# An allowance between a transfer's planned landing and its readers in the list schedule of a transformer block's end

## The chip, the cores and the metric

The kernel runs on one core of one Trainium2 chip. The metric is device time in microseconds (us), the median of several runs. The core's engines are TensorE (PE in the profile; its weight loads are PEld), VectorE (DVE), ScalarE (ACT), GpSimd (POOL) and SyncE (SP), which issues nearly all transfers (DMA). Each engine takes its instructions strictly in the order in which the program lists them, so an instruction that waits holds up everything behind it on its engine.

## The reference

One block with adaptive layer normalisation on a sequence of 2048 tokens of 512 features, all in float32: sliding-window attention (32 heads of 16, window 256), then a gated feed-forward layer of width 1792.

```python
mod = (_silu(c) @ w_mod).reshape(c.shape[0], 6, 1, -1)
sa, ca, ga, sb, cb, gb = (mod[:, i] for i in range(6))
h = _layernorm(x) * (1 + ca) + sa
x = x + ga * attention(h, wqkv, wo)        # 32 heads, causal, window 256, softmax
h = _layernorm(x) * (1 + cb) + sb
x = x + gb * ((_silu(h @ w1) * (h @ w3)) @ w2)
```

## The kernel before

Every float32 product is made of three reduced-precision products: each operand is split into a rounded part and the rest ("cutting": ScalarE copies the rounded part, VectorE or POOL subtracts it). Attention runs as 32 units (8 groups of four heads by 4 row blocks of 512 tokens), each laid out by a hand-made table of times. In a unit TensorE makes scores twice: once for the row maxima (L485 into the banks `mx`, reduced by VectorE at L494), once transposed for the probabilities (L753 into `st`); VectorE merges masks into a score tile (L773) or adds them (L761), ScalarE takes the exponential (L766, L768), POOL masks (L780), and TensorE multiplies by the values (L721). The maxima go back through DRAM-like rows (L517) into the queries' extra rows. A unit's sums and values leave through `os` (L815) to DRAM (L818, `o_dr`).

What comes after the planned time TS, the last units and all that follows, is not written out by hand. The function builds a list of operations, each with an engine, an assumed duration, a key and its dependences, and `Sched.deal` deals them out greedily: at every step it starts, over all engines, the operation that can start first, and on one engine the ready operation with the smallest key. The units' remaining operations are `fixed`: they take their engine at their planned times `us(t)`. The order in which `deal` picks is the order of the program; its times are used nowhere else. Its costs are constants: RATE (transfer speed) and QUIET (how close a transfer may come to an urgent one), TW (how planned unit times are stretched), PEM (an allowance between a result of ACT, DVE or POOL and its reader on TensorE) and DM. DM is an allowance between the landing of a transfer and its reader on any engine but SyncE, and holds only while fixed unit operations are left. `late` (in `deal`) selects these readers, and the last lines of the loop add the allowance:

```python
m = PEM if u.eng == "PE" and o.eng in ("ACT", "DVE", "POOL") else DM if late(o, u, s) else 0.0
u.est = max(u.est, s + (o.lat + m if u.eng != o.eng or o.kb else o.occ))
```

What is dealt, in the words of the prediction:

- Row sums (`o_sums`): for each row block the sums of 24 heads (tile `wqr`, 96 rows) and of the last 8 (tile `mT`, 32 rows) are loaded from `o_dr` (L1068), inverted by VectorE (L1072) and stored to `r_dr` (L1073).
- Pieces (`o_part`): four per row block. The values are loaded (L1092), the inverted sums are spread over them by a load (L1087), multiplied (L1104), rounded (L1096) and subtracted (L1099). `K["by"]` says for each piece whether VectorE or POOL multiplies and subtracts. The second row block's cut pieces lie in a tile named `x1b`, the others' in `o`.
- Projection (`o_proj`, L1116), the residual add with the row sum on VectorE (L985), the sum of squares on ScalarE (L993), the root on POOL (L1007).
- Normalised rows and their transposes for the first half of the tokens (L1236, L1250 on TensorE, L1254), and their sums, differences and cuts (L1267, L1273, L1275), which are the seven operands `b` of a Strassen-like product of 2 x 2 blocks.
- The feed-forward layer: 14 units (2 halves of the tokens by 7 slices). A unit has 14 *ups* (L1378, six matmuls each) with adds on VectorE and POOL (L1409, L1421), gates (L1401, L1405) and cuts (L1449, L1452), and 8 *downs* (L1471, six matmuls each) that VectorE adds to the residual (L1476). The weights are loaded by L1174 and cut by L967 and L968. The second half's normalised rows are transposed in between (L1302, L1311, L1315). The keys of all of it come from the table K.

Of the kernel before, what the change touches and what calls it, by code (L numbers as in the profile page):

```python
# [112 lines left out]
class Sched:  # L113
# [36 lines left out]
    def deal(self):  # L150
# [17 lines left out]
        while left:  # L168
            best = None
            for e, lst in ready.items():  # L170
                t, pick = free[e], None
                for key, seq, o in lst:
# [10 lines left out]
                    if o.kb:  # L183

                        b = max(s, t)
                        end = max(wire, b + 1.5) + o.kb / RATE + o.more - QUIET
                        s = max([s] + [u + 0.01 for u in self.urgent if b <= u < end])
# [36 lines left out]
            if o.kb:  # L224
                s = max(s, lanes.pop(0))
                wire = max(wire, s + 1.5) + o.kb / RATE + o.more
                o.lat = wire + 0.4 - s
# [17 lines left out]
            for u in o.users:  # L245
                m = PEM if u.eng == "PE" and o.eng in ("ACT", "DVE", "POOL") else DM if late(o, u, s) else 0.0
                u.est = max(u.est, s + (o.lat + m if u.eng != o.eng or o.kb else o.occ))
# [6 lines left out]

INORDER = ("up",)
INF = float("inf")
RATE = 320.0

QUIET = 1.487
KEY = 1.715  # L260
TS = 229.9

# [1 line left out]
def us(t):  # L264

    return KEY * (min(t, TW[0]) - TS + TW[2] * max(0.0, min(t, TW[1]) - TW[0]) + TW[3] * max(0.0, t - TW[1]))


TW = (231.0, 241.0, 0.8, 0.583)

KINDS = dict(product=("PE", 0.235), mix=("POOL", 1.25), qk_rows=("SP", 0.65), out=("ACT", 0.5), job=("POOL", 2.0),
             job_dma=("SP", 0.5), scores=("PE", 0.19), top=("DVE", 0.5), parts=("DVE", 0.4), turn=("PE", 0.11), cut=("ACT", 0.16),
# [1 line left out]
             far=("PE", 0.125), part=("POOL", 0.92), side=("ACT", 0.53), far_side=("ACT", 0.27), side_mask=("POOL", 0.92),  # L274
             side_probs=("ACT", 0.53), values=("PE", 0.66), cut_all=("ACT", 0.48), store=("SP", 0.45))
NPE = 3
PEM = 0.998
DM = 0.076

BY = ((("POOL", "POOL"),) * 3 + (("DVE", "DVE"),), (("POOL", "POOL"),) * 3 + (("DVE", "DVE"),),  # L280
      (("POOL", "DVE"),) * 3 + (("DVE", "DVE"),), (("POOL", "POOL"),) * 4)
K = dict(be=(('POOL', 'DVE'), ('POOL', 'DVE'), ('DVE', 'POOL'), ('POOL', 'POOL'), ('POOL', 'POOL'),
         ('POOL', 'POOL'), ('DVE', 'POOL')), hr=2.855, de=12.48, wo=-3.567, x1=16.6, xb=-38.041, xl=-26.167,
         os=-0.13, ol=(-17.833, -5.162, -9.509, 10.002), pl=(11.205, -2.398, -4.869, 102.62), pe=(0.914, -2.635,
         56.103, 231.635), o=(2.337, 8.384, 18.214, 9.324), n=(1, 1, 2, 1), w0=67.715, l2=2.802, f=2.068,
         fl=40.1, by=((('POOL', 'POOL'), ('DVE', 'DVE'), ('DVE', 'POOL'), ('DVE', 'DVE')), (('DVE', 'DVE'),
         ('DVE', 'POOL'), ('DVE', 'POOL'), ('DVE', 'DVE')), (('POOL', 'POOL'), ('DVE', 'DVE'), ('DVE', 'POOL'),
         ('POOL', 'DVE')), (('DVE', 'POOL'), ('DVE', 'POOL'), ('DVE', 'POOL'), ('DVE', 'POOL'))), w=-2.134,
         dn=1.412, ds=0.003, l3=-10.82)

@with_exitstack
def block_kernel(ctx: ExitStack, tc: tile.TileContext, x, wqk, wv, wo, w13, w2, c, wmod, out):
# [1313 lines left out]
```

## Time and profile before

| | us |
|---|---|
| median of 3 runs | 954.08 (952.42 to 954.97) |
| the profiled execution | 952.06 |
| its span, first to last instruction | 950.3 |
| TensorE busy in the span | 916.3 (96%) |
| VectorE, ScalarE, POOL busy | 670.0, 525.1, 545.6 |
| mean granted clock of TensorE | 0.982 |

In the rows below, a window's row gives its length, then for each engine its busy us (and instructions), the granted TensorE clock, the mean busy share of the 16 DMA engines and GB/s. A row in order of time gives start, duration, engine, line, operation, what it writes and reads, and in brackets how long the engine stood idle before it and what ended that. "SPq" is SyncE issuing a transfer.

### The profile page before, as it was taken

To read this page: it belongs to the slowest core of one execution; us is meant where nothing else is said; L and a number is where in the kernel's file an instruction comes from. 1 tells how busy PE (TensorE), PEld (TensorE's weight loads), DVE (VectorE), ACT (ScalarE), POOL (GpSimd) and SP (SyncE) were. 2 spreads that over 40 slices of the span, in tenths; PEclk is the share of its full clock that TensorE was granted. 3 is DMA by queue.
4 is the path that set the end of the run, shared out by engine and by line. 5 is a ranking of instruction groups with operands and counts; after the bars stand their busy time and mean duration, and the time that the engine had idled before them with its cause. 6 is when DMAs were issued, how large, how long until landed. Compare 5 with 4: busy or idle time off the path is not lost.

```text
span 950.3 us, 16719 instructions
## 1 busy us (share of the span) xinstructions
PE 916.3 (96%) x5330; PEld 710.3 (75%) x5330; DVE 670.0 (71%) x1861; ACT 525.1 (55%) x1031; POOL 545.6 (57%) x694
## 2 busy tenths in 40 slices
PE   5999999999999999988987999999999999999998
PEld 3688677777777777755765878888888888888886
DVE  7675789888898989876668565665558645566465
ACT  3333777777777777766577754333455334433330
POOL 6220566676757566645566789977659546453420
PEclk9999899999999999988989999999999999999999
DMA  8621465555655555565960659645244512323002
GB/s 296 200 80 46 113 185 163 158 146 164 183 156 150 170 157 147 136 183 167 298 220 12 221 199 322 222 171 166 90 161 157 187 41 99 99 62 97 26 23 89
DMA packets 125020, 141.62 MB, mean 149 GB/s; under 512 B 60034, under 2 KB 72834, under 8 KB 124932
## 3 DMA queue, kind: packets, MB, share of 16 engines
q1 hardware_dynamic: 124212, 139.51, 48.0%
q10 hardware_dynamic: 720, 1.05, 0.3%
q8 instruction: 42, 0.69, 0.3%
q14 instruction: 46, 0.38, 0.1%
HBM read 85.72 MB, written 34.61 MB: 127 GB/s over the span
## 4 chain that ended last, share of the span: by engine, by line
PE 78%; DVE 6%; DMA 4%; POOL 4%; ACT 3%; issue 2%; SPq 2%; POOLq 0%; DVEq 0%; ACTq 0%
PE st L1378 11%; PE mx L1378 10%; PE pj L438 8%; PE st L753 8%; PE mx L485 8%; PE po L721 8%; PE st L1471 7%; PE mx L1471 7%; PE st L653 5%; PE pj L1378 3%; PE pj L1471 2%; DMA r_dr<-mT 1%; DVE t L1267 1%; DVE b L1275 1%; DMA qk<-o_dr 1%
## 5 line engine op out<-in xcount | busy, mean ns | idle before, releaser
L494 DVE CUSTOM_DVE_ANT_0 junk<-mx,mskq 128x320 bf16<-128x320 f32 (+4 forms) x512 | 223.4, 464 | 39.6 <-PE mx L485 39.0
L968 POOL TENSOR_TENSOR w<-w,w 128x512 fp32r<-128x512 f32 (+2 forms) x56 | 107.0, 1924 | 111.6 <-ACT w L967 61.8
L485 PE MATMUL mx<-ringk,ringq 96*128 96x320 f32 (+4 forms) x512 | 154.9, 326 | 2.2 <-DVE mt L494 2.2
L753 PE MATMUL st<-ringq,ringk 98*128 98x256 f32 (+1 forms) x528 | 141.9, 338 | 6.8 <-DVE st L773 2.5
L780 POOL TENSOR_SCALAR_AFFINE_SELECT pt<-pt 128x256 f32<-128x256 f32 x224 | 92.4, 413 | 74.7 <-ACT pt L768 67.0
L438 PE MATMUL pj<-hT,wq 128*128 128x512 f32 x384 | 132.5, 403 | 0.3 <-DVE wq L427 0.3
L485 PEld LDWEIGHTS mx<-ringk,ringq 96*128 96x128 f32 x512 | 98.6, 193 | 41.4 <-DVE mt L494 23.1
L768 ACT ACTIVATE pt<-st 128x512 f32<-128x512 f32 (+1 forms) x198 | 115.2, 587 | 24.7 <-DVE st L773 10.5
L753 PEld LDWEIGHTS st<-ringq,ringk 98*128 98x128 f32 x528 | 91.8, 194 | 22.2 <-ACT pt L768 5.8
L721 PE MATMUL po<-pt,vS 128*17 128x384 f32 (+2 forms) x1408 | 92.7, 394 | 0.0
L438 PEld LDWEIGHTS pj<-hT,wq 128*128 128x128 f32 x384 | 68.4, 192 | 7.8 <-DVE wq L427 0.8
L1378 PE MATMUL st<-b,w 128*128 128x512 f32 x270 | 67.8, 391 | 1.3 <-ACT t L1412 1.3
L1409 DVE TENSOR_TENSOR t<-st,t 128x512 f32<-128x512 f32 x48 | 33.0, 688 | 43.3 <-PE st L1378 28.5
L1409 DVE TENSOR_TENSOR t<-mx,t 128x512 f32<-128x512 f32 x49 | 33.5, 687 | 41.8 <-PE mx L1378 28.0
L721 PEld LDWEIGHTS po<-pt,vS 128*17 128x17 f32 x1408 | 34.6, 98 | 36.3 <-issue 19.8
L1449 ACT ACTIVATE wq<-g 128x512 fp32r<-128x512 f32 x28 | 17.7, 631 | 77.2 <-DVE g L1405 38.1
L1378 PE MATMUL mx<-b,w 128*128 128x512 f32 x240 | 59.9, 389 | 0.0
L773 DVE COPY_PREDICATED st<-later,st 128x256 f32<-128x256 uint8 x112 | 47.5, 424 | 17.3 <-PE st L753 12.7
L1378 PEld LDWEIGHTS st<-b,w 128*128 128x128 f32 x270 | 50.5, 188 | 12.1 <-ACT t L1412 1.7
L795 POOL TENSOR_SCALAR_AFFINE_SELECT sm<-sm 128x256 f32<-128x256 f32 x109 | 42.3, 406 | 29.5 <-ACT sm L785 28.6
L761 DVE TENSOR_TENSOR st<-st,mskr 128x256 f32<-128x256 f32 x125 | 53.6, 429 | 8.0 <-PE st L753 8.0
L967 ACT ACTIVATE w<-w 128x512 fp32r<-128x512 f32 (+2 forms) x56 | 42.5, 786 | 20.7 <-DMA w<-wsum 11.2
(256 smaller groups left out, 2010.6 us busy)
## 6 DMA issues: line engine op xcount, KB each, us to landing
ringq<-qk SPq DMA_DIRECT2D x192, 64.0 KB
ringk<-qk SPq DMA_DIRECT2D x96, 128.0 KB
o_dr<-os SPq DMA_DIRECT2D x32, 256.0 KB
w<-wsum SPq DMA_DIRECT2D x14, 512.0 KB
w<-w2g SPq DMA_DIRECT2D x14, 512.0 KB
jb<-in_w SPq DMA_DIRECT2D x24, 256.0 KB
wraw<-in_w SPq DMA_DIRECT2D x7, 768.0 KB
w<-wraw SPq DMA_DIRECT2D x14, 384.0 KB
```

The lines of the kernel that those rows point to most:

```text
L438: nc.tensor.matmul(v["ps"], WQ[g][w][:, n // 3], hTp(i, n // 3, b * BT, BT), start=(n == 0), stop=(n == 3 * KC - 1))
L485: nc.tensor.matmul(v[i][:, :n], both_queries(a, gs), keys(NS, a, (gs + 1) * HP - n, n), start=True, stop=True)
L494: nc.vector.tensor_tensor_reduce(out=junk[:, :n], in0=v[i][:, :n], in1=mskq[:, WK - n:], scale=1.0, scalar=-3e38, op0=ALU.add, op1=ALU.max ...
L721: nc.tensor.matmul(po[32 * i:32 * i + DH + 1, qb * P:(qb + nq) * P], vS[:, kb, 4 * g + i], pts[i // 2][:, i % 2, c0:c0 + nq], start=first, ...
L753: nc.tensor.matmul(o, keys(NM, a, kb * P, P), queries(a, q, n), start=q == lo, stop=not plus and q + n == hi, skip_group_check=True)
L761: nc.vector.tensor_tensor(out=ps, in0=ps, in1=mskk[:, p:p + 1].to_broadcast([P, 2, P]), op=ALU.add)
L768: nc.scalar.activation(held[u, j, a][:, :, :n], v[j, a, 0].rearrange("p (h q) k -> p h q k", h=2)[:, :, :n], AF.Exp, scale=SCALE)
L780: nc.gpsimd.affine_select(out=pt[:, :, 2 * m], in_=pt[:, :, 0], **w)
L968: sch.op(eng, lambda: on_eng(eng).tensor_tensor(out=lo(), in0=src(), in1=hi().bitcast(F32), op=ALU.subtract), 0.06 + 0.0024 * n if eng == ...
L1378: nc.tensor.matmul(ps(bk), WT[s, n][w][:, col], BB[t, k][r], start=start and c == 0, stop=stop and c == 5, skip_group_check=True)
L1409: return nc.vector.tensor_add(o, x, y)
L1471: nc.tensor.matmul(ps(bk), tiles[hk + (h,)][:, i * P:(i + 1) * P], w2_of(last, y, f), start=(m == 0), stop=(m == 5))
```

## The change

Only constants change: DM from 0.076 to 3.359, PEM from 0.998 to 1.262, RATE from 320.0 to 299.475, QUIET and TW a little, and in K nearly all keys and the choice between VectorE and POOL. The work is the same, and so are the attention units before TS. What moves is the order that `deal` makes of the end, on all engines.

```diff
-RATE = 320.0
-QUIET = 1.487
+RATE = 299.475
+QUIET = 1.657
...
-TW = (231.0, 241.0, 0.8, 0.583)
+TW = (231.0, 241.0, 0.8, 0.611)
...
-PEM = 0.998
-DM = 0.076
+PEM = 1.262
+DM = 3.359
...
-         ('POOL', 'POOL'), ('DVE', 'POOL')), hr=2.855, de=12.48, wo=-3.567, x1=16.6, xb=-38.041, xl=-26.167,
+         ('POOL', 'DVE'), ('DVE', 'POOL')), hr=-6.211, de=0.969, wo=-6.368, x1=4.266, xb=-12.052, xl=-14.242,
...
-         56.103, 231.635), o=(2.337, 8.384, 18.214, 9.324), n=(1, 1, 2, 1), w0=67.715, l2=2.802, f=2.068,
+         55.497, 233.263), o=(6.308, 9.841, 14.839, 13.354), n=(2, 1, 1, 1), w0=80.926, l2=5.192, f=3.484,
```

Three places of the order. On VectorE, the first reciprocal of row sums (L1072), before; L494 is a row maximum of an attention unit and L773 a mask merge:

```order
L494 ISA junk,mt<-mx,mskq 128x320
L494 ISA mt 128x1
L761 TENSOR_TENSOR st<-st,mskr 128x256
L1072 RECIPROCAL wqr<-wqr 96x128
L773 COPY_PREDICATED st<-later,st 128x2x128
```

and the rows in front of it now, where L502 and L503 close a unit's maxima:

```order
L502 TENSOR_SCALAR mr<-mt 128x16
L503 SCALAR_TENSOR_TENSOR mr<-mt,mr 128x16
L494 ISA junk,mt<-mx,mskq 128x320
L494 ISA mt 128x1
L773 COPY_PREDICATED st<-later,st 128x2x128
L494 ISA junk,mt<-mx,mskq 128x320
L494 ISA mt 128x1
L494 ISA junk,mt<-mx,mskq 128x320
L494 ISA mt 128x1
L1072 RECIPROCAL wqr<-wqr 96x128
```

The reciprocal moved from row 1347 to row 1375 of VectorE, past 11 maxima; the first one of a 32-row tile moved from row 1390 to row 1403, past 6. On SyncE the load of the first one's data stands where it stood.

Again on VectorE, after the last unit's maxima, before:

```order
L773 COPY_PREDICATED st<-later,st 128x2x128
L1072 RECIPROCAL wqr<-wqr 96x128 x2
L773 COPY_PREDICATED st<-later,st 128x2x128
L1104 TENSOR_TENSOR qk_7400<-qk_7400,qk_7413 128x512
L773 COPY_PREDICATED st<-later,st 128x2x128
L1104 TENSOR_TENSOR wq_7426<-wq_7426,wq_7447 128x512
```

and now:

```order
L1072 RECIPROCAL wqr<-wqr 96x128 x2
L773 COPY_PREDICATED st<-later,st 128x2x128
L1104 TENSOR_TENSOR qkr<-qkr,qk_7410 128x512
L773 COPY_PREDICATED st<-later,st 128x2x128
L1104 TENSOR_TENSOR qk_7361<-qk_7361,qk_7425 128x512
L1104 TENSOR_TENSOR wq_7394<-wq_7394,wq_7450 128x512
L773 COPY_PREDICATED st<-later,st 128x2x128
```

The first row block's first product (`qkr`), which POOL had, has come to VectorE, between the merges.

On TensorE, the last two downs (L1471) of the second feed-forward unit, before:

```order
L1471 MATMUL st<-w_7799,qkr 128x512
L1471 MATMUL st<-w_7800,qkr 128x512
L1471 MATMUL st<-w_7799,qk_8808 128x512
L1471 MATMUL st<-w_7799,qk_8745 128x512
L1471 MATMUL st<-w_7800,qk_8745 128x512
L1471 MATMUL st<-w_7799,qk_8751 128x512
L1471 MATMUL mx<-w_7799,qkr 128x512
```

and now:

```order
L1471 MATMUL st<-w_7784,qk_8850 128x512
L1378 MATMUL mx<-b_7776,wo_8251 128x512
L1378 MATMUL mx<-b_7776,wo_8252 128x512
L1378 MATMUL mx<-b_7777,wo_8251 128x512
L1378 MATMUL mx<-b_7778,wo_8251 128x512
L1378 MATMUL mx<-b_7778,wo_8252 128x512
L1378 MATMUL mx<-b_7779,wo_8251 128x512
L1471 MATMUL pj<-w_7784,qkr 128x512
```

An up stands between them. Before, eight downs follow fourteen ups in nearly every unit; now a unit's order is eight ups, three or four downs, and then ups and downs by turns. Both end with the last 16 downs.

More of the change, by code (lines that the diff above doesn't have):

```diff
@@ L282 @@
 K = dict(be=(('POOL', 'DVE'), ('POOL', 'DVE'), ('DVE', 'POOL'), ('POOL', 'POOL'), ('POOL', 'POOL'),
-         ('POOL', 'POOL'), ('DVE', 'POOL')), hr=2.855, de=12.48, wo=-3.567, x1=16.6, xb=-38.041, xl=-26.167,
-         os=-0.13, ol=(-17.833, -5.162, -9.509, 10.002), pl=(11.205, -2.398, -4.869, 102.62), pe=(0.914, -2.635,
-         56.103, 231.635), o=(2.337, 8.384, 18.214, 9.324), n=(1, 1, 2, 1), w0=67.715, l2=2.802, f=2.068,
[L286 to L289, printed above, removed]
+         ('POOL', 'DVE'), ('DVE', 'POOL')), hr=-6.211, de=0.969, wo=-6.368, x1=4.266, xb=-12.052, xl=-14.242,
+         os=2.058, ol=(-15.53, -11.029, -7.444, 0.822), pl=(5.2, -14.242, -17.703, 101.932), pe=(1.564, -3.906,
+         55.497, 233.263), o=(6.308, 9.841, 14.839, 13.354), n=(2, 1, 1, 1), w0=80.926, l2=5.192, f=3.484,
+         fl=37.767, by=((('DVE', 'DVE'), ('DVE', 'DVE'), ('DVE', 'POOL'), ('DVE', 'DVE')), (('POOL', 'DVE'),
+         ('DVE', 'DVE'), ('POOL', 'DVE'), ('POOL', 'POOL')), (('DVE', 'DVE'), ('DVE', 'DVE'), ('DVE', 'DVE'),
+         ('POOL', 'DVE')), (('DVE', 'POOL'), ('DVE', 'POOL'), ('DVE', 'DVE'), ('DVE', 'POOL'))), w=3.067,
+         dn=1.899, ds=0.094, l3=-18.084)
 @with_exitstack
```

## The prediction

> **What bounds the kernel now.** I read the page first, then the busy time by stages, then TensorE's and VectorE's rows in order of time where a stage was not full.
>
> ```profile
> span 950.3 us, 16719 instructions
> core 0: us, PE busy (x) PEld busy (x) DVE busy (x) ACT busy (x) POOL busy (x), PEclk, DMA share, GB/s
> 404.00:460.00 56.00, 50.15 (x369) 31.86 (x371) 38.58 (x132) 34.36 (x77) 26.07 (x45) 0.88 0.66 193
> 460.00:480.00 20.00, 20.00 (x108) 16.11 (x100) 14.06 (x28) 12.60 (x24) 12.88 (x8) 1.00 0.98 302
> 480.00:520.00 40.00, 30.92 (x126) 23.34 (x125) 31.36 (x44) 28.17 (x52) 25.27 (x18) 0.87 0.29 100
> 520.00:560.00 40.00, 38.95 (x182) 31.35 (x182) 23.16 (x35) 30.18 (x50) 30.52 (x26) 1.00 0.55 180
> 560.00:946.00 386.00, 385.44 (x1701) 318.62 (x1699) 228.95 (x318) 149.00 (x234) 223.21 (x165) 1.00 0.39 130
> ```
>
> The planned end begins near 404 us. From 560 to 946 us TensorE is busy for 385.44 of 386 us at full granted clock: that part is bound by TensorE's own work, and since the change adds and removes no matmul, it can only get worse. What can be won lies between 404 and 560 us: 5.85 us idle to 460, 9.08 us from 480 to 520, 1.05 us to 560, and the clock that falls to 0.88 and 0.87 around the idle stretches. Before 404 us nothing is changed. TensorE's longest waits in these stretches, with what released them:
>
> ```profile
> 417.19 0.39 PE L753 MATMUL st<-ringq,ringk 98*128 98x256 f32 x1 [0.58 <-ACT pt L766]
> 419.78 0.58 PE L753 MATMUL st<-ringq,ringk 98*128 98x256 f32 x1 [2.06 <-DVE st L773]
> ...
> 436.24 1.46 PE L485 MATMUL mx<-ringk,ringq 96*128 96x320 f32 x3 [1.95 <-DVE mt L494]
> ...
> 483.36 0.48 PE L1250 MATMUL mx<-ident,wqr 128*128 128x128 f32 x1 [2.98 <-ACT wqr L1236]
> ...
> 505.66 1.76 PE L1116 MATMUL mx<-wo,o 128*128 128x512 f32 x6 [2.68 <-ACT t L1254]
> ...
> 514.29 1.66 PE L1378 MATMUL st<-b,w 128*128 128x512 f32 x6 [1.26 <-ACT t L1412]
> ...
> 519.24 1.20 PE L1116 MATMUL pj<-wo,o 128*128 128x512 f32 x4 [1.46 <-POOL o L1099]
> ```
>
> Two of them, 2.06 and 1.95 us, end with VectorE work of the attention units. VectorE's own rows say why it was late:
>
> ```profile
> 418.45 0.95 DVE L1072 RECIPROCAL wqr<-wqr 96x128 f32<-96x128 f32 x1 [1.74 <-DMA wqr<-o_dr]
> 419.32 0.40 DVE L773 COPY_PREDICATED st<-later,st 128x256 f32<-128x256 uint8 x1
> ...
> 420.45 0.48 DVE L494 CUSTOM_DVE_ANT_0 junk<-mx,mskq 128x320 bf16<-128x320 f32 x1
> 420.87 0.08 DVE L494 DVE_READ_ACCUMULATOR2_ANT mt<- 128x1 f32 x1
> 420.87 0.48 DVE L494 CUSTOM_DVE_ANT_0 junk<-mx,mskq 128x320 bf16<-128x320 f32 x1
> ...
> 434.89 0.94 DVE L1072 RECIPROCAL mT<-mT 32x128 f32<-32x128 f32 x1 [1.74 <-DMA qkr<-o_dr]
> ```
>
> Twice a reciprocal of the softmax sums, which no attention unit needs, stands at the head of VectorE's queue for 1.74 us until its data have come from DRAM. Behind it stand the mask merge (L773) and the maxima (L494) for which TensorE waits.
>
> **The change part by part.** (1) *The allowance.* DM goes from 0.076 to 3.359 us, and readers of a transfer are planned that much later while units run. The order shows it acting: the first reciprocal now has 11 more maxima ahead of it, at one start per 0.42 us (420.45 to 420.87) at least 4.6 us; the one of the 32-row tile has 6 more, 2.5 us. Both exceed the 1.74 us waited. So I take both waits as gone: 2.06 + 1.95 = 4.01 us. Their lower bound is nothing, if the load or the store before it is later too; the order leaves the first load where it was.
>
> The half clock that follows goes with them:
>
> ```profile
> 416.00:420.00 4.00, 1.36 (x7) 0.82 (x5) 2.26 (x6) 1.14 (x3) 0.00 (x0) 0.79 0.51 122
> 420.00:424.00 4.00, 4.00 (x14) 3.31 (x14) 3.23 (x16) 2.41 (x6) 2.26 (x6) 0.50 0.93 284
> 424.00:428.00 4.00, 3.78 (x34) 2.08 (x34) 2.42 (x11) 2.63 (x7) 1.99 (x4) 0.85 0.75 253
> 428.00:432.00 4.00, 3.97 (x39) 2.61 (x39) 2.91 (x12) 3.23 (x8) 3.93 (x6) 1.00 0.28 95
> 432.00:436.00 4.00, 2.29 (x13) 1.59 (x12) 2.26 (x8) 1.85 (x4) 0.80 (x1) 0.93 0.73 212
> 436.00:440.00 4.00, 3.76 (x16) 2.53 (x20) 3.67 (x18) 1.98 (x4) 2.82 (x5) 0.50 0.89 275
> 440.00:444.00 4.00, 3.88 (x28) 2.03 (x21) 1.36 (x3) 1.82 (x5) 2.05 (x3) 0.72 0.04 10
> ```
>
> Busy time times the missing share of the clock: after the first wait 1.36 x 0.21 + 4.00 x 0.50 + 3.78 x 0.15 = 2.86 us, after the second 2.29 x 0.07 + 3.76 x 0.50 + 3.88 x 0.28 = 3.13 us, together 5.99 us. Part 1 is worth 4.01 + 5.99 = 10.0 us at most, and that is what I take.
>
> The Trainium skill bears on the half of this that is clock. "TensorE: Matmul & The Clock Gate", Part 1, has the clock halved after an idle window of about 3.4 us, at a phase that is not the kernel's own, and restored after about as long a busy one. By its number alone waits of 2 us would leave the clock up, and part 1 would be worth 4.0 us. The rows here have 0.50 behind each of the two waits, so the trace differs and decides.
>
> (2) *Products moved to VectorE.* Over the four row blocks 4 of the 32 multiplications and subtractions go from POOL to VectorE, and the first row block's first one, which POOL waited for, now stands on VectorE between the merges of the last unit.
>
> ```profile
> 436.03 1.27 POOL L1104 TENSOR_TENSOR qkr<-qkr,qk 128x512 f32<-128x512 f32 x1 [3.23 <-DMA qk<-r_dr]
> ...
> 449.43 0.68 DVE L1104 TENSOR_TENSOR wq<-wq,wq 128x512 f32<-128x512 f32 x1
> 450.20 0.94 DVE L1072 RECIPROCAL mT<-mT 32x128 f32<-32x128 f32 x1
> ...
> 486.36 2.85 DVE L1104 TENSOR_TENSOR wq<-wq,wq 128x512 f32<-128x512 f32 x1
> ```
>
> Four at 0.68 us are 2.7 us if all lie on the path, nothing if all fall into VectorE's waits. I take one, 0.7 us, the one that merges stand behind. (2.85 us is the same form beside POOL's weight cuts; four of those would be 11.4 us, and I don't take it, because the moved ones are not all there.) The wait for the spread, 3.23 us on POOL, comes onto VectorE between 0 and 3.2 us; nearer to 0, since the product now stands behind both of the last reciprocals (two of 0.94). I take 1.0 us.
>
> (3) *The transfers behind.* If attention ends 10.0 us earlier, its outputs must come back from DRAM 10.0 us earlier too. The queue ran at a share of 0.98 in 460 to 480 us, so it can move only by what it idled before: (1 - 0.28) x 4 + (1 - 0.04) x 4 = 6.7 us in the two windows in which SyncE stood behind the rows that the stalls made late. That leaves 3.3 us short. The second row block's last piece was ready some 2.2 us before TensorE began it:
>
> ```profile
> 465.75 0.68 DVE L1099 TENSOR_TENSOR x1b<-wq,x1b 128x512 fp32r<-128x512 f32 x1
> ...
> 468.66 8.32 PE L1116 MATMUL st<-wo,x1b 128*128 128x512 f32 x36
> ```
>
> (465.75 + 0.68 to 468.66). So 3.3 - 2.2 = 1.1 us is given back; the ends are 0 and the whole 10.0.
>
> (4) *Normalisation and the first ups, 480 to 520 us.* The keys move here too: between the two groups of transposes 48 projection matmuls stand instead of 36, and fewer after. In all the same work fills the same chain of ScalarE, VectorE and POOL, so the 9.08 us of idle time stay in my sum. Either way I allow one wait such as the largest, 2.98 us.
>
> (5) *Feed-forward.* Down products no longer stand in blocks of eight; in the first half of a unit they alternate with ups. The matmuls are the same, and TensorE had no idle time there, so nothing can be won. I take 0. The price if a wait appears is the one stretch of before in which ups are mixed with other work:
>
> ```profile
> 548.95 1.66 PE L1378 MATMUL mx<-b,o 128*128 128x512 f32 x6 [0.24 <-DVE t L1409]
> 551.20 1.66 PE L1378 MATMUL st<-b,wo 128*128 128x512 f32 x6 [0.60 <-ACT t L1416]
> ...
> 553.51 1.66 PE L1378 MATMUL st<-b,wo 128*128 128x512 f32 x6 [0.21 <-DVE t L1409]
> ```
>
> That is 1.05 us in one unit; in twelve mixed units 12.6 us. RATE, QUIET, PEM and TW cost nothing themselves: they set only the order. The end is the same 16 downs, their adds and stores.
>
> Sum: -10.0 + 0.7 + 1.0 + 1.1 + 0 + 0 = -7.2 us against the profiled execution's 952.06 us (its span of 950.3 us and 1.8 us around it), so 944.9 us. The median of the runs is 954.08 us, 2.02 us above that execution: 946.9 us.
>
> **The rivals.** *The transfers take it back* (chance 0.16). The transfers of 460 to 480 us run at a share of 0.98; if their end does not move, the 10.0 us return as waits at the first normalisation: 954 to 955 us. Against it: the 6.7 us of idle queue ahead of it.
>
> *Mixed downs make TensorE wait* (0.17), the one on the slower side. A unit's conversions must follow the last down of the unit before, which now comes after six ups instead of before the first. If the chain ACT, DVE, POOL that frees the banks for the next eight ups is then late, each of twelve units waits. It decides from 7.2 / 12 = 0.6 us a unit on; at the 1.05 us of the mixed stretch the time is 946.9 + 12.6 = 959.5 us. Against it: VectorE is busy for 228.95 of 386 us and ScalarE for 149.00, and eight ups in a row follow.
>
> *More than forecast* (0.13): the normalisation loses its 2.98 us wait and the moved products cost nothing, 946.9 - 2.98 - 1.7 = 942.2 us. For it: less of the second block's products stands in front of the last row sum. Against: two still do, and one of that form took 2.85 us.
>
> *The clock stays low without the waits* (0.05): the half clock comes from the thin matmuls of the last units. Then 5.99 us stay, 952.9 us. The clock of 1.00 in 428 to 432 us, between the two waits, speaks against it. [...]
>
> *The allowance does nothing* (0.06): other keys put the loads as much later as the readers. 954 us. The order of SyncE, where the first load keeps its place, speaks against it.
>
> **How the numbers follow.** The forecast has the remaining 0.43, with its own range of 943.5 to 950.5 us (part 2 fully hidden or fully paid, part 3 at 0 or 3.3). This kernel's measurement tells a difference from none at about 0.3%, 2.9 us. Faster: 0.43 + 0.13, and 0.04 of the undecided rest, 0.60. Within 0.3%: 0.16 + 0.05 + 0.06 less those 0.04, 0.23. Slower: 0.17. The range from 940.5 to 957.5 us leaves out the slower case at its full price and little else.
>
> **What would show it.** Right: no wait of VectorE at L1072 over 0.3 us between 404 and 450 us; TensorE's granted clock near 1.00 up to 450 us; the last attention matmul (L721) some 9 us earlier than 461 us; and TensorE full from the first ups on. Part 3 wrong: new waits at L1116 with DMA behind them. Part 5 wrong: TensorE busy for less than 99% in any 40 us after 560 us. The forecast fails if the reciprocals still wait, or if the time won before 460 us is idle time between 460 and 530 us.

## The result and the profile after

The changed kernel takes 944.57 us (median; 940.54 to 945.38) against 953.25 us for the kernel before beside it: a ratio of 0.990, 95% interval 0.987 to 0.993. The forecast was 946.9 us. The profiled execution took 944.52 us, with a span of 942.8 us, 7.5 us less than before. In a later comparison, beside some of the experiments, the changed kernel took 944.87 us and the kernel before 950.71 us: 0.993 (0.990 to 0.996). So it is faster, by something between 0.4 and 1.3%; both comparisons are used below.

The same stretches as in the prediction, of the changed kernel:

```profile
span 942.8 us, 16694 instructions
core 0: us, PE busy (x) PEld busy (x) DVE busy (x) ACT busy (x) POOL busy (x), PEclk, DMA share, GB/s
404.00:460.00 56.00, 50.20 (x373) 32.70 (x370) 40.66 (x130) 35.42 (x76) 25.79 (x42) 0.94 0.68 197
460.00:480.00 20.00, 17.48 (x74) 13.70 (x73) 16.36 (x31) 13.66 (x25) 13.01 (x8) 0.95 0.98 291
480.00:520.00 40.00, 37.57 (x166) 29.81 (x166) 27.86 (x55) 31.01 (x59) 19.21 (x15) 0.94 0.40 133
520.00:560.00 40.00, 37.45 (x169) 29.91 (x168) 26.33 (x28) 26.10 (x39) 32.35 (x30) 0.96 0.49 158
560.00:938.00 378.00, 378.00 (x1670) 312.86 (x1670) 236.88 (x312) 146.24 (x233) 214.13 (x161) 1.00 0.40 130
```

Two things stand out. The feed-forward from 560 us on is full, as before. And 404 to 460 us is not: TensorE is idle for 5.80 of 56 us, as long as before (5.85), and the clock is 0.94 rather than 0.88. The stretch in which the prediction saw the whole gain has lost no idle time, although the reciprocals wait no more. They stand in VectorE's rows without a wait:

```profile
422.56 0.94 DVE L1072 RECIPROCAL wqr<-wqr 96x128 f32<-96x128 f32 x1
429.60 0.94 DVE L1072 RECIPROCAL wqr<-wqr 96x128 f32<-96x128 f32 x1
434.32 0.93 DVE L1072 RECIPROCAL mT<-mT 32x128 f32<-32x128 f32 x1
```

TensorE's longer waits, after the change:

```profile
428.39 0.48 PE L753 MATMUL st<-ringq,ringk 98*128 98x256 f32 x2 [2.31 <-DMA ringq<-mT]
430.95 0.63 PE L485 MATMUL mx<-ringk,ringq 96*128 96x320 f32 x1 [0.64 <-DVE mt L494]
...
476.94 0.33 PE L1250 MATMUL mx<-ident,wqr 128*128 128x128 f32 x1 [1.56 <-ACT wqr L1236]
...
499.96 3.35 PE L1116 MATMUL mx<-wo,o 128*128 128x512 f32 x12 [0.58 <-ACT t L1254]
...
519.15 1.65 PE L1378 MATMUL mx<-b,w 128*128 128x512 f32 x6 [1.65 <-ACT t L1416]
...
544.90 1.93 PE L1378 MATMUL st<-b,wo 128*128 128x512 f32 x6 [2.44 <-DVE t L1409]
```

The 2.06 and 1.95 us behind VectorE are gone, and a wait of 2.31 us with a transfer behind it is new: `ringq<-mT`, the 16 KB of the maxima's rows (L517). SyncE's rows show what stands ahead of it:

```profile
418.06 1.50 SPq L1053 DMA_DIRECT2D x1a<-in_x  x3
419.60 1.85 SPq L1047 DMA_DIRECT2D wo<-wog  x4
421.50 1.70 SPq L1068 DMA_DIRECT2D wqr<-o_dr  x2
423.30 0.69 SPq L517 DMA_DIRECT2D ringq<-mT  x1
```

The rows are issued at 423.30 us and let TensorE go at 428.39, 5.1 us later, behind three residual and four weight loads of 256 KB each. In the kernel before, the stall had held the same issue back to 427.53 us (4.2 us later, of which 1.5 us is a later start of the whole), when the loads had drained (a DMA share of 0.28 in 428 to 432 us). The transfer had been covered by the stall that the change removed.

### The profile page after: what moved, and what is told of

It is laid out like the page before. It is cut to its first block, busy times and chain, and to the rows that moved or that the text cites. A ratio compares the mean times of both kernels' runs of the same rounds, so it can differ in the third digit from the quotient of the medians.

```text
span 942.8 us, 16694 instructions
## 1 busy us (share of the span) xinstructions
PE 913.9 (97%) x5330; PEld 707.8 (75%) x5330; DVE 683.9 (73%) x1866; ACT 524.2 (56%) x1031; POOL 533.8 (57%) x689
## 3 DMA queue, kind: packets, MB, share of 16 engines
q10 hardware_dynamic: 720, 1.05, 0.4%
## 4 chain that ended last, share of the span: by engine, by line
PE 86%; DVE 5%; ACT 4%; DMA 2%; issue 1%; POOL 1%; SPq 0%; POOLq 0%; ACTq 0%; DVEq 0%
PE mx L1378 11%; PE st L1378 11%; PE pj L438 9%; PE st L753 9%; PE po L721 8%; PE mx L485 8%; PE mx L1471 7%; PE st L1471 7%; PE st L653 5%; PE pj L1378 3%; PE pj L1471 3%; PE mx L1116 1%; DVE t L1267 1%; PE st L631 1%; DMA wo<-wog 1%
## 5 line engine op out<-in xcount | busy, mean ns | idle before, releaser
L494 DVE CUSTOM_DVE_ANT_0 junk<-mx,mskq 128x320 bf16<-128x320 f32 (+4 forms) x512 | 223.4, 465 | 37.6 <-PE mx L485 36.9
L968 POOL TENSOR_TENSOR w<-w,w 128x512 fp32r<-128x512 f32 (+2 forms) x56 | 98.5, 1774 | 54.7 <-ACT w L967 46.8
L1378 PE MATMUL st<-b,w 128*128 128x512 f32 x276 | 68.7, 390 | 0.0
L1421 POOL TENSOR_TENSOR t<-t,t 128x512 f32<-128x512 f32 x28 | 37.5, 1339 | 50.3 <-DVE t L1409 50.3
L1378 PE MATMUL mx<-b,w 128*128 128x512 f32 x240 | 60.4, 390 | 1.6 <-ACT t L1416 1.6
L773 DVE COPY_PREDICATED st<-later,st 128x256 f32<-128x256 uint8 x112 | 47.5, 424 | 18.8 <-PE st L753 16.4
L1378 PEld LDWEIGHTS st<-b,w 128*128 128x128 f32 x276 | 51.7, 188 | 11.0 <-ACT t L1416 0.3
L967 ACT ACTIVATE w<-w 128x512 fp32r<-128x512 f32 (+2 forms) x56 | 42.8, 786 | 30.6 <-DMA w<-wraw 16.5
L1378 PEld LDWEIGHTS mx<-b,w 128*128 128x128 f32 x240 | 44.8, 188 | 11.5 <-ACT t L1416 2.1
```

The lines of the kernel that those rows point to most:

```text
L494: nc.vector.tensor_tensor_reduce(out=junk[:, :n], in0=v[i][:, :n], in1=mskq[:, WK - n:], scale=1.0, scalar=-3e38, op0=ALU.add, op1=ALU.max ...
L773: nc.vector.copy_predicated(bank(j, a, 0), later, bank(j, a, 1))
L968: sch.op(eng, lambda: on_eng(eng).tensor_tensor(out=lo(), in0=src(), in1=hi().bitcast(F32), op=ALU.subtract), 0.06 + 0.0024 * n if eng == ...
L1378: nc.tensor.matmul(ps(bk), WT[s, n][w][:, col], BB[t, k][r], start=start and c == 0, stop=stop and c == 5, skip_group_check=True)
```

## Where the time went

Start-up differs from one execution to the next, before anything that the change touches: by 1.5 us between the two kernels' traces, and by up to 3.1 us over all traces here (the mark below lies between 409.28 and 412.34 us). To leave it out, I count from a mark that all kernels share: the copy of an attention unit's output (L815) at 411.58 us in the kernel before, the last one ahead of any difference (it stands 10.6 us behind its predecessor in every trace). The copy of the last unit's output ends "attention"; "the rest" is from there to the span's end. For the kernel before:

```profile
411.58 0.59 ACT L815 ACTIVATE os<-po 128x512 f32<-128x512 f32 x1
...
461.22 0.60 ACT L815 ACTIVATE os<-po 128x512 f32<-128x512 f32 x1
```

So 49.64 us of attention and 950.3 - 461.22 = 489.08 us of rest. For the changed kernel:

```profile
410.07 0.59 ACT L815 ACTIVATE os<-po 128x512 f32<-128x512 f32 x1
...
456.21 0.60 ACT L815 ACTIVATE os<-po 128x512 f32<-128x512 f32 x1 [0.24 <-ACT x1b L1096]
```

46.14 and 486.59 us. The table gives both parts as differences from before, for one profiled execution of each kernel; the ratio is that of the timed runs. The last column is TensorE's idle time plus busy time times the missing clock, summed over windows of 2 us from 404 to 556 us; before, it is 26.24 us.

| kernel | ratio, 95% interval | attention | rest | sum | idle + clock loss |
|---|---|---|---|---|---|
| changed | 0.990 (0.987–0.993) | -3.50 | -2.49 | -5.99 | 13.32 + 7.85 |
| changed, again | 0.993 (0.990–0.996) | -2.24 | -4.13 | -6.37 | 13.76 + 6.03 |
| allowance alone | 0.9928 (0.9912–0.9943) | -4.24 | -2.51 | -6.75 | 14.11 + 4.68 |
| changed, allowance as before | 0.9957 (0.9941–0.9973) | +1.05 | -4.02 | -2.97 | 16.13 + 9.33 |
| reciprocals alone, by hand | 0.9981 (0.9966–0.9995) | -2.57 | -1.59 | -4.16 | 15.82 + 6.03 |
| the same, residual late | 1.0005 (0.9989–1.0020) | +1.43 | -1.28 | +0.15 | 16.37 + 8.65 |
| changed, bulk loads late | 0.9930 (0.9916–0.9945) | -4.37 | -3.11 | -7.48 | 12.98 + 4.57 |
| changed, residual later | 0.9927 (0.9909–0.9946) | -4.28 | -3.78 | -8.06 | 11.59 + 6.21 |
| changed, residual last | 0.9917 (0.9888–0.9945) | -4.70 | -2.64 | -7.34 | 10.91 + 8.00 |
| changed, downs in blocks | 0.9919 (0.9889–0.9949) | -4.27 | -4.53 | -8.80 | 11.76 + 6.49 |
| residual last, downs in blocks | 0.9915 (0.9897–0.9933) | -7.35 | -3.40 | -10.75 | 11.14 + 4.31 |
| product table alone | 1.0069 (1.0049–1.0089) | +1.90 | +5.88 | +7.78 | 18.17 + 12.63 |
| mixed downs alone | 0.9997 (0.9981–1.0012) | +0.65 | +1.26 | +1.91 | 17.60 + 9.91 |

Two executions of the same changed kernel differ by 1.3 us in one part and 1.6 us in the other, so single entries are good to about 2 us. What the traces show is not one gain of 10 us in attention, but about 3 us there and about 3 us behind it.

## Experiments: the allowance against the other keys

The theory (T) after comparing the traces: the allowance removes VectorE's two waits, about half of it comes back as the wait for the rows, and the other keys bring the rest in the normalisation. The rival (R): the gain is the other keys', and the allowance only shifts waits.

**The allowance alone.**

```diff
 # kernel before
-DM = 0.076
+DM = 3.359
```

> The kernel before (953.25 us) with the allowance alone (DM 3.359), every other key as before. Theory T (the allowance takes VectorE's two waits of 1.74 us away, and about half of what TensorE wins comes back as a wait for the maxima's rows): 3.5 us less, 948 to 951 us, no wait at L1072 before 450 us, and a wait of about 2.3 us on a score matmul with DMA ringq behind it. Theory R (the gain is in the other keys, the allowance only shifts it): 952 to 954 us. The prediction's own sum for the allowance, -10.0 + 1.1 us: 944 us.

Measured: 945.06 against 951.21 us, 0.9928. R falls. T put the share of the allowance at 3.5 us, and it is 6.2 us, as much as the whole change gained in the later comparison (5.8 us). The first reciprocal has no transfer to wait for, and the one wait of TensorE above 0.7 us before 450 us is shorter than the two that it replaces:

```profile
421.53 0.63 PE L485 MATMUL mx<-ringk,ringq 96*128 96x320 f32 x1 [1.11 <-DVE mt L494]
```

The wait for the rows that T expected does not come. They are issued at 427.03 us, which is 15.10 us behind the mark against 15.95 us before and 13.23 us in the changed kernel, and some 4 us after the last of the weight loads. So T was wrong about what follows here. The allowance also holds back other readers of transfers than the reciprocals: ScalarE makes its first conversion of a weight (L967) only at 429.71 us, behind the unit's output copy, and waits for no load.

```profile
429.71 1.18 ACT L967 ACTIVATE wo<-wo 128x512 fp32r<-128x512 f32 x2
```

**The change without the allowance.**

```diff
 # changed kernel
-DM = 3.359
+DM = 0.076
```

> The changed kernel (944.57 us) with the allowance set back to 0.076 us, the other keys as changed. Theory T: the part of the allowance, 3.5 us, is lost: 947 to 950 us, and VectorE waits again at L1072 for about 1.7 us. Theory R: 943 to 946 us, as the changed kernel. The prediction's sum (all of the gain is the allowance's, the moved products cost 1.7 us): 954 to 956 us.

Measured: 947.66 us, 0.9957. Both waits of VectorE at L1072 are back:

```profile
419.19 0.95 DVE L1072 RECIPROCAL wqr<-wqr 96x128 f32<-96x128 f32 x1 [1.80 <-DMA wqr<-o_dr]
...
436.51 0.94 DVE L1072 RECIPROCAL mT<-mT 32x128 f32<-32x128 f32 x1 [1.22 <-DMA mT<-o_dr]
```

Attention ends 1.05 us later than in the kernel before. Yet the kernel is 3.5 us faster than before, all of it behind attention (-4.02 us). So the other keys are worth 3.5 us without the allowance, and the allowance is worth 6.2 us without them. By the comparison that follows, together they are worth about what the allowance brings alone: the two do not add up, against the part of T that divided the gain between them. Which of the other keys wins behind attention was not tested: of those tried alone below, the product table loses and the down keys change nothing.

**The changed kernel beside these.**

> The changed kernel once more, so that it stands beside the others on one chip. Theory T: 0.990 of the kernel before; if the allowance alone (0.993 of before) were the whole of the gain, 0.993; if the other keys add what they brought without the allowance (0.9957), 0.988 to 0.989.

Measured: 0.993, equal to the allowance alone (0.9928); the interval, 0.990 to 0.996, does not exclude 1 or 2 us beside it. It does exclude 0.9885, the product of the two ratios above. The first comparison, of four runs each (0.987 to 0.993), would allow that product, so that the two do not add up rests on the later one. In this execution the wait for the rows is 2.86 us rather than 2.31.

## Experiments: where a removed wait goes

**The reciprocals alone.** The order of before, edited by hand: the first reciprocal goes behind 11 more maxima and the one of the 32-row tile behind 6 more, each with its store. TensorE, ScalarE and POOL keep their order.

```diff
-    order = sch.deal()
+    order = edit(sch.deal(), marks, {id(fn): kind for _, _, fn, kind in last})
...
+    past(marks["rec", 0, 0], marks["back", 0, 0], 11)
+    past(marks["rec", 0, 6], marks["back", 0, 6], 6)
```

> The order of the kernel before, with two things moved by hand: the first reciprocal of the row sums goes behind 11 more maxima, the one of the 32-row tile behind 6 more, each with the store that follows it. TensorE, ScalarE and POOL keep their order. Theory T: TensorE's waits of 2.06 and 1.95 us with VectorE behind them go, the maxima's rows are issued about 4 us earlier, behind the early residual and weight loads, and land late: a new wait of about 2.3 us with DMA behind it; 3 to 4 us less in all, 949 to 950.5 us. The prediction's part 1 and 3: 10.0 - 1.1 us less, 944 us. Theory R: no more than 1 us from 953.25 us.

Measured: 949.12 us, 0.9981. The waits behind VectorE are gone, and the one that takes their place is neither of those expected. The chain behind it, first on TensorE, then on ScalarE:

```profile
426.98 0.50 PE L753 MATMUL st<-ringq,ringk 98*128 98x512 f32 x1 [3.54 <-ACT pt L768]
```

```profile
424.67 0.63 ACT L967 ACTIVATE wo<-wo 128x512 fp32r<-128x512 f32 x1 [4.10 <-DMA wo<-wog]
```

ScalarE reaches the conversion of the first weight (L967) earlier and stands 4.10 us for its load, which has four residual loads ahead of it; the probabilities that TensorE needs are queued behind. The stall at the reciprocal had covered this too. With the allowance alone, and in the changed kernel, ScalarE makes that conversion behind the unit's output copy (L815); the move by hand left it ahead. So the moved reciprocals bring 2.1 us of the median, and the allowance 6.2 us. That other readers which the allowance holds back, such as this conversion, make up the rest is likely, but no run shows it alone.

**The same, with the residual behind.**

```diff
+    for t in (4, 5, 6, 7):
+        f = marks["x1", t]
+        order.remove(f)
+        order.insert(order.index(marks["sums", 0, 6]) + t - 3, f)
```

> The order of before with the reciprocals put back by hand as in the run before, and with the four early residual loads behind the load of the 32-row tile, so that the weights, which ScalarE waited 4.10 us for, come first. Theory T: TensorE's wait of 3.54 us behind ScalarE goes, and no wait above 1 us is left before 450 us: 6 to 9 us less than before, ratio 0.990 to 0.994. Theory Q: another wait of 2 us or more takes its place, ratio 0.997 to 0.999 as with the reciprocals alone.

Measured: 951.51 us, 1.0005: nothing is left of the gain. ScalarE waits 1.56 us for its weights rather than 4.10, but now the residual loads stand ahead of the spread of the reciprocals, for which POOL waits with the masks of the next unit queued behind it:

```profile
437.87 1.26 POOL L1104 TENSOR_TENSOR qkr<-qkr,qk 128x512 f32<-128x512 f32 x1 [7.68 <-DMA qk<-r_dr]
```

```profile
440.02 1.05 PE L721 MATMUL po<-pt,vS 128*17 128x256 f32 x8 [4.73 <-POOL pt L780]
```

The wait of POOL was 3.23 us in the kernel before and cost nothing; at 7.68 us it stops TensorE for 4.73.

**The changed kernel with bulk loads late.** Three steps, each moving loads back in SyncE's order alone. In the first, two weight loads and three residual loads go behind the rows and the store of that unit, where the fourth residual load stands already (1.28 MB of the 1.79 MB ahead of the rows).

```diff
+    late = []
+    for m in (("wo", 2), ("wo", 3), ("x1", 4), ("x1", 5), ("x1", 6)):
+        f = marks[m]
+        order.remove(f)
+        at = [i for i, g in enumerate(order) if kinds.get(id(g)) == "store"][0] + 1 + len(late)
+        order.insert(at, f)
+        late.append(f)
```

> The changed kernel with five of the seven early loads (three of the residual, two of the weights, 1.28 MB) moved behind the rows of the maxima and the store of that unit in SyncE's order; nothing moves on another engine. Theory T (the rows land 5.0 us after their issue because these loads are in the queue ahead of them): the rows land in about 2.5 us, TensorE's wait of 2.31 us and the 0.64 us after it go, with about 3 us of half clock: 939 to 942 us. A rival Q (the queue is the bound up to 480 us, and what is moved back comes as a wait further on): 944 to 946 us. A rival S (the rows' time is not the queue's): the wait of 2.31 us stays, 944.5 us.

Measured: 944.78 us, 0.9930. The rows are issued at 423.01 us, and TensorE does not wait for them: the 2.31 us were the loads ahead. But the next small transfer pays. SyncE's order is now this:

```profile
423.01 0.69 SPq L517 DMA_DIRECT2D ringq<-mT  x1
423.75 0.41 SPq L818 DMA_DIRECT2D o_dr<-os  x1
424.20 0.95 SPq L1047 DMA_DIRECT2D wo<-wog  x2
425.19 1.87 SPq L1053 DMA_DIRECT2D x1a<-in_x  x4
...
429.31 0.71 SPq L1068 DMA_DIRECT2D mT<-o_dr  x1
```

The 32-row tile of sums, 16 KB, is issued at 429.31 us, and its reader starts at 434.75, 5.4 us later:

```profile
434.75 0.94 DVE L1072 RECIPROCAL mT<-mT 32x128 f32<-32x128 f32 x1 [2.07 <-DMA mT<-o_dr]
```

TensorE then waits 1.51 us behind VectorE at 436.07 us. The Trainium skill's "DMA: Bandwidth & Descriptors", in "Queues, rings and completion order", has each DMA engine consume the descriptors of one queue in the order in which they were issued. These traces agree: 16 KB take 5.1 and 5.4 us behind bulk loads, and the same 16 KB of rows are not waited for once those loads are issued behind them.

In the second step the four residual loads go behind that tile's load as well; the edit is that of the run before.

> The changed kernel with two weight loads behind the store of that unit, as in the run before, and the four residual loads further back, behind the load of the 32-row tile of row sums, which came 5.4 us after its issue there. Theory T (each small transfer on the attention's path pays for the loads queued ahead of it): neither the maxima's rows (2.31 us of TensorE's wait) nor the 32-row tile (1.51 us) is waited for, and 2 to 3 us of half clock go with them: 3 to 5 us less than the changed kernel. Theory Q (the queue is the bound, so a load put back stalls another reader): no more than 1 us from it. A loss of more than 1 us would mean that the residual now comes too late for its own readers.

Measured: 943.39 us, 0.9927. Attention keeps its end (-4.28 us), because the wait moves once more, to the rows of the last unit:

```profile
440.88 0.47 PE L753 MATMUL st<-ringq,ringk 98*128 98x256 f32 x2 [1.36 <-DMA ringq<-mT]
```

In the third step they go behind the last unit's rows, store and sums too (`marks["sums", 1, 6]` in the place of `marks["sums", 0, 6]`).

> The changed kernel with two weight loads behind the first late store, and the four residual loads that the second row block needs behind the rows, the store and the sums' load of the last unit but none, so that no early bulk load stands ahead of any of the small transfers of attention. In the runs before, each step back moved the wait: 2.31 us for the rows of one unit, then 1.51 us for the 32-row tile, then 1.36 us for the rows of the last unit (440.88 us). Theory T: the last of these goes too, with some 3 us of half clock at 440 to 450 us: 3 to 4 us less than with the loads one step earlier (0.9927 of before), 0.989. Theory Q: the wait moves once more, to the second row block's products or to the first normalisation, 0.992 to 0.994.

Measured: 943.48 us, 0.9917. No wait above 0.71 us is left before 450 us, and idle time between 404 and 460 us falls from 5.80 to 3.60 us. But the clock loses 3.22 us there, as in the changed kernel (3.09), and the first normalisation waits 1.41 us. The timed difference from the changed kernel stays below what the intervals tell apart. So by their medians all three steps lie nearer the rival Q, though the last interval (0.9888 to 0.9945) does not exclude T's 0.989. The rows show that T's mechanism is real, and that each of the first two steps moved its price on to the next reader.

## Experiments: the other parts

**Mixed downs alone.**

```diff
 # kernel before, in K
-dn=1.412, ds=0.003
+dn=1.899, ds=0.094
```

> The kernel before with the two keys of the down products alone (dn 1.899, ds 0.094), which mix downs with ups in each feed-forward unit. The prediction's part 5: no more than 1 us from before. Its rival: 1.05 us in each of 12 units, 12.6 us more. A third way: the 0.77 us that TensorE idled between 552 and 920 us go and the normalisation is not touched: 0.5 to 1 us less.

Measured: 0.9997. Mixing costs nothing that can be measured. In the profile TensorE is busy for 384.48 of the 386 us from 560 to 946 us, against 385.44 before; one wait of 1.5 us at L1378 is most of the difference.

**The changed kernel with downs in blocks** (the same two keys the other way round).

> The changed kernel with the two keys of the down products set back (dn 1.412, ds 0.003), so that downs stand in one block per unit again. The prediction's part 5: no more than 1 us from the changed kernel (0.993 of before on this chip). A rival: the wait of 2.44 us in the first mixed unit (544.90 us, VectorE at L1409) is the price of the mixing, and without it the time is 2 to 3 us less, 0.990 to 0.991.

Measured: 943.06 us, 0.9919. The wait of 2.44 us at 544.90 us is gone, so under the changed keys the mixing has that one price, in the first mixed unit (with the keys of before, mixed downs alone show no such wait). It is in part exchanged: before a projection matmul at 497.45 us TensorE now waits 2.34 us for ScalarE (L1254), where the two traces of the changed kernel have 0.58 and 1.24 us. The median is about 1.5 us below the changed kernel's 944.6 and 944.9 us, which is within the intervals.

**The product table alone** (`by` of the changed kernel in the kernel before).

> The kernel before with the table of product engines alone (by), which puts the first row block's first product on VectorE. The prediction's part 2: 0.7 us for the product and 1.0 us for its wait for the spread, 1.7 us more, 1.002. A rival: TensorE's wait for VectorE gets longer by the whole 3.23 us that POOL waited, with the clock 5 us or more, 1.005. Another: the first row block's outputs come earlier, no loss or a gain, 0.998 to 1.000.

Measured: 958.14 us, 1.0069, the largest move of all. Not where it was expected: VectorE's first product has no transfer to wait for.

```profile
447.47 0.69 DVE L1104 TENSOR_TENSOR qkr<-qkr,qk 128x512 f32<-128x512 f32 x1
```

The loss is in the projection of the last row block, whose pieces come late from POOL and ScalarE when the engines change and the keys don't:

```profile
506.04 0.50 PE L1116 MATMUL pj<-wo,o 128*128 128x512 f32 x1 [2.25 <-POOL o L1099]
...
514.89 1.22 PE L1116 MATMUL pj<-wo,o 128*128 128x512 f32 x2 [4.77 <-ACT o L1096]
```

Neither wait stands in the changed kernel. What the table costs under the changed keys was not run by itself.

**Both edits that stood under the changed kernel together:** residual last and downs in blocks.

> The changed kernel with both edits that stood under it: downs in one block per unit again (0.9919 of before alone) and the bulk loads behind the small transfers of attention (0.9917 alone), against 0.990 and 0.993 for the changed kernel. If the two add up, which touch other stretches (404 to 450 us and 520 to 560 us): 0.989 or less, 940 to 941 us, TensorE without a wait above 1 us before 450 us and none of 2.4 us at 544 us. If they don't (the first normalisation takes back what attention wins): 0.991 to 0.993.

Measured: 942.84 us, 0.9915. Its profile is the one in which attention comes nearest to the forecast:

```profile
404.00:450.00 46.00, 42.32 (x339) 26.62 (x332) 35.78 (x125) 32.23 (x71) 22.96 (x43) 1.00 0.72 213
450.00:460.00 10.00, 9.87 (x61) 7.03 (x60) 8.02 (x13) 5.05 (x12) 4.58 (x4) 1.00 0.78 235
460.00:480.00 20.00, 17.18 (x67) 13.18 (x66) 14.89 (x26) 14.46 (x27) 13.99 (x9) 0.86 0.94 261
```

The clock is 1.00 through 460 us and attention ends 7.35 us earlier than before. That profiled execution, 940.62 us, is the fastest of this kernel, though, and the median is 2.2 us above it. The waits went as expected, none above 1 us before 450 us and none of 2.4 us at 544 us; by the median the two edits do not add up, and 0.989 lies just outside the interval (0.9897 to 0.9933). Whether this version beats the changed kernel (0.990 and 0.993) is not settled by these intervals.

## Why the prediction came out

The time was right, 946.9 us forecast and 944.57 us measured, inside the likeliest case's own range. Its sum was not: -10.0 + 0.7 + 1.0 = -8.3 us in attention, where the moved product stands, and +1.1 us behind it. Two traces of the changed kernel show -3.5 and -2.2 us in attention and -2.5 and -4.1 us behind it. Two errors of opposite sign made the total come out near, which is luck. The measured change itself is -8.7 us in the first comparison and -5.8 us in the later one, on either side of the -7.2 us forecast. The range of 943.5 to 950.5 us does not follow from the ends named for it either: parts 2 and 3 at their ends (0 to 2.7 + 3.2 us, and 0 to 3.3 us) give 944.1 to 953.3 us.

**Part 1, the allowance.** That the allowance removes both waits at the reciprocals is right: they go with it alone, and return when it is set back. It alone brings 6.2 us, where the reciprocals moved by hand, with both waits gone too, bring only 2.1 us. The size is wrong. The step that failed is "Part 1 is worth 4.01 + 5.99 = 10.0 us at most, and that is what I take": the upper end was taken as the value. The check behind it asked only whether the reciprocal itself would still wait. It did not ask what else the stall covered; in the changed kernel that was the rows at L517, issued 2.7 us earlier (counted from the mark) behind 1.79 MB of loads that stood ahead of them before as well. With no early bulk load ahead of attention's small transfers, and the downs in blocks, attention gains 7.35 us, near the forecast. The run with the residual last alone, which has the same order of loads in attention, gains 4.70 us: TensorE idles as long up to 460 us (3.60 and 3.80 us), but one execution loses 3.22 us to the clock there and the other nothing. So the 7.35 us need a lucky clock as well.

**Clock near 1.00 to 450 us** failed: it is 0.72 in 428 to 440 us, behind the new wait. **The last attention matmul 9 us earlier** failed: 461 to 456 us, of which 1.5 us is start-up. **TensorE full from the first ups on** failed too: waits of 1.65 and 2.44 us stand at L1378.

**Part 2, products on VectorE,** +1.7 us: not paid in the changed kernel, where the first product, like the one quoted above, stands at 442.51 us without a wait. The table alone delays attention by 1.90 us, but the trace puts most of that on TensorE's clock (8.10 us lost in 404 to 460 us against 5.72 before; 6.57 us idle against 5.84), not on the product: agreement in the number only.

**Part 3, transfers give back 1.1 us:** no wait with DMA behind it at L1116 in the changed kernel, though the queue's share is again 0.98 in 460 to 480 us. With attention 7.35 us earlier the first normalisation still waits no longer than before (2.14 us against 2.98). The rival that let the transfers take everything back there falls. They do take back, but elsewhere: in attention, not at the projection.

**Part 4, the normalisation, 0 ± 2.98 us:** mis-sized, inside its bounds. TensorE idles 7.52 and 7.75 us from 460 to 556 us in the two traces of the changed kernel, against 10.13 before: 2.5 us won. The four waits of 2.98, 2.68, 1.46 and 1.26 us before are three of 1.56, 0.58 and 1.65 us now, with the 2.44 us of the first mixed unit as a fourth. The clock loss in the same stretch, 4.55 us before, is 0.2 us more in the one trace of the changed kernel and 3.0 us less in the other; two executions of one order cannot owe that to the order. What won the 2.5 us among the keys was not tested.

**Part 5, mixed downs, 0:** right but for one unit. TensorE is busy for all of 560 to 938 us, and the two keys alone leave the time where it was. The rival of 1.05 us in each of twelve units falls; one unit, the first, has a wait of 2.44 us where the kernel before has 1.05 us.

**The other rivals.** "The allowance does nothing" falls with the run of the allowance alone. "The clock stays low without the waits" is not settled. In the last run the same thin matmuls ran at 1.00. In the run with the residual last, with the same order in attention, the clock was 0.50 in 420 to 422 us, though TensorE had no wait above 0.59 us in the 10 us before (the rows are in the last section). So part of the half clock can stay when the long waits are gone. "More than forecast" was right in part: the first normalisation waits 1.4 us less (2.98 to 1.56), and the first moved product does not wait. It failed with part 1, on which it rested.

## What to carry to other kernels

Before you book a stall as won, list every transfer and conversion that the stall gave time to, and place each at its earlier time in its queue: here a 2 us wait of VectorE had covered a 5.1 us transfer, a 4.10 us wait of ScalarE and a wait of POOL, and each came out as the one above it was removed. Take the upper bound of a gain only when the next constraint in the row has been priced. Terms of a schedule that were fitted together need not add up. Here the allowance alone brought 6.2 us, all the other keys 3.5 us, both together 5.8 us in the later comparison, and one table alone lost 6.6 us (0.7%).

## What the runs showed of the hardware

What a wait costs in clock does not follow from its length. The same wait in two executions of the changed kernel, 2.44 and 2.43 us at L1378, the first:

```profile
544.00:548.00 4.00, 3.10 (x12) 2.55 (x13) 2.23 (x4) 2.70 (x6) 2.85 (x5) 0.76 0.17 66
548.00:552.00 4.00, 4.00 (x18) 3.25 (x17) 0.69 (x1) 1.49 (x3) 1.55 (x4) 0.81 0.42 149
```

and the second:

```profile
544.00:548.00 4.00, 2.18 (x12) 1.83 (x13) 2.89 (x5) 2.89 (x6) 2.03 (x4) 1.00 0.17 66
548.00:552.00 4.00, 4.00 (x21) 3.29 (x20) 0.95 (x2) 2.19 (x4) 2.44 (x6) 1.00 0.27 103
```

3.10 x 0.24 + 4.00 x 0.19 = 1.5 us in the one, nothing in the other. With the allowance alone, 1.11 us of waiting was followed by half clock:

```profile
420.00:422.00 2.00, 0.89 (x4) 0.57 (x4) 1.83 (x6) 1.00 (x2) 1.12 (x3) 0.59 0.88 263
422.00:424.00 2.00, 2.00 (x15) 0.80 (x18) 1.39 (x7) 0.87 (x2) 0.41 (x1) 0.50 0.89 264
424.00:426.00 2.00, 2.00 (x19) 1.12 (x11) 0.11 (x1) 0.60 (x1) 0.41 (x1) 0.50 0.95 261
426.00:428.00 2.00, 2.00 (x10) 1.57 (x8) 1.64 (x6) 0.74 (x2) 0.00 (x0) 0.70 0.83 310
```

0.89 x 0.41 + 2.00 x (0.50 + 0.50 + 0.30) = 3.0 us. With the reciprocals alone, 3.54 us of waiting cost 1.02 x 0.08 + 2.00 x 0.50 + 2.00 x 0.27 = 1.6 us:

```profile
426.00:428.00 2.00, 1.02 (x6) 0.98 (x7) 0.21 (x1) 2.00 (x5) 2.00 (x3) 0.92 0.26 97
428.00:430.00 2.00, 2.00 (x23) 1.14 (x26) 1.20 (x6) 1.67 (x4) 1.93 (x4) 0.50 0.32 105
430.00:432.00 2.00, 2.00 (x17) 0.80 (x9) 1.28 (x2) 0.00 (x0) 1.19 (x1) 0.73 0.43 109
```

With the residual last, where TensorE had stood idle for 0.63 us in 416 to 418 us and 0.03 us in the next two, the clock fell all the same (both traces of the changed kernel have the same wait, 0.57 and 0.58 us, and keep the full clock behind it): 1.97 x 0.18 + 2.00 x 0.50 + 2.00 x 0.17 = 1.7 us:

```profile
418.00:420.00 2.00, 1.97 (x10) 1.42 (x8) 1.70 (x8) 1.74 (x4) 1.58 (x5) 0.82 0.50 121
420.00:422.00 2.00, 2.00 (x17) 0.67 (x20) 1.05 (x5) 0.87 (x2) 1.05 (x3) 0.50 0.89 232
422.00:424.00 2.00, 2.00 (x23) 1.28 (x14) 0.76 (x3) 0.86 (x2) 0.08 (x1) 0.83 0.26 86
```

The Trainium skill's "TensorE: Matmul & The Clock Gate", Part 1, has the gate watch windows of a clock of its own that does not begin with the kernel, so that the cost varies from run to run; the two executions above agree. An idle window of 3.4 us, which it asks for, is not what these rows show: half clock began behind waits of 1.11 and 2 us, and once behind 0.6 us of idle time. The changed kernel's own times beside the experiments lie between 939.38 and 947.24 us; that the clock makes up all of this spread was not shown. In a stretch of short waits the clock's half of a gain is thus an expectation, and should not be taken at its full size from one profile.
